# An mLSTM with two feed-forward layers: sign of the weight words placed by ScalarE, a finer order of steps, and the second layer's first pair in other banks

## Chip, cores, metric

One Trainium2 chip, one of its cores. The metric is the device time of one execution in microseconds (us), the median of the runs; the profile is of one execution.

## What is computed

Three stages follow each other, all in float32 with a precision that needs split products:

```python
# 1. a gated recurrence over 768 steps, 2 batches x 8 heads, head size 40
C = f * C + i * outer(v, k);  n = f * n + i * k
y = sigmoid(o) * (C @ q) / max(|n . q|, 1)
# 2. x: 1536 x 320 (all heads side by side)
h = max(max(x @ w1, x @ w2), x @ w3)        # 320 x 768 each
x = h @ w_out                                # 768 x 320
# 3.
h = x @ w_in                                 # 320 x 2048
g = h * tanh(softplus(h))                    # "mish"
out = g @ w_out2                             # 2048 x 320
```

The weights come in as 64-bit floats, two 32-bit words each; the kernel makes 32-bit floats of them on the chip.

## The kernel before

**Recurrence.** Steps are cut into 6 chunks of 128, times 2 batches: 12 units, numbered `u`, even units batch 0 and odd ones batch 1. A unit's steps have one-letter names: `F` spreads forget gates by TensorE into a PSUM bank, `D` scans them on VectorE into decays `dt`, `S` are the scores q.k (TensorE, `sc`), `X` multiplies both (VectorE), `V`, `K`, `Q` scale values, keys and queries (GpSimd or VectorE), `N` is the numerator (TensorE, `it`), `den`, `sg`, `xn` divide and gate, `T` transposes (`xp`), `xh` and `xl` are the high and low part of the result, which the first layer reads in three blocks of four units. `O` is the new part of the state (TensorE, `sp`), `sd` and `C` update the state `st`.

**First layer.** For each block, `P:blk,m,i` makes one of 18 products of 8 matmuls in the banks m0 to m2 (`mm`), `t` takes the maximum over three of them into `zraw` (ScalarE the first, VectorE the others), `hh` and `hl` split it; `d` multiplies by the output weights into the banks m0 to m2 (`mz`), `e` moves these out on ScalarE, two of them by L610 and the third by two moves to `sw` (L613, L614) and an addition on VectorE.

**Second layer.** For three blocks of 512 rows and 8 pairs of 128 columns each, `expand` makes the halves of a pair (`h`), `mish` evicts it twice on ScalarE (`gh`, `g`) with a subtraction on VectorE (`gl`), and two pairs later `contract` multiplies into four banks o0 to o3 (`o`).

**Weights.** A slab is 128 x 640 words of 64 bits: 9 slabs `w` (first layer), 3 `o`, 8 `i` and 8 `p` (second layer). `fet` loads a slab into one of three `raw` buffers, `sc` scales the two words on ScalarE (`dec` from the high word, and the low word in place), `mg` merges on VectorE in two instructions (L492 the digits, L494 the sign), `rd` rounds to the high part on ScalarE, `cut` makes the low part, on GpSimd or VectorE. The last five slabs (`LATE`: i7 and p4 to p7) are decoded while the second layer runs.

**Order.** `PLAN` is a written list of steps; it fixes the order on every engine and on SP's queue (all DMAs) up to the end of the first layer. Step names, numbers and, after @, the PSUM banks stand in it. From there a second fixed order holds for TensorE alone. Each engine works its queue in order, so whatever stands ahead in a queue must be finished first. PSUM banks c0, c1, s0, s1, s2 belong to the recurrence and become mx and o0 to o3 of the second layer when it is over. Where a step names no bank, `O` and `N` take s0. In `hbank` (L678) the pair's tiles `h` take mx for every fourth column and else m0, m1, m2 in turn, so the first pair takes m1 and mx.

The lines that matter below: L333 `D`, L352 `X`, L383 and L385 `N`, L465 `C`, L485 and L486 `sc`, L492 and L494 `mg`, L515 to L520 `rd`, L610 to L614 `e`, L678 `hbank`, L698 every matmul of the second layer.

Of the kernel before, what the change touches and what calls it, by code (L numbers as in the profile page):

```python
# [8 lines left out]
F32 = mybir.dt.float32  # L9
F32R = mybir.dt.float32r  # L10
AF = mybir.ActivationFunctionType
ALU = mybir.AluOpType
# [61 lines left out]
def mlstm_moe_kernel(ctx, tc, fi0, fir, qk2, q3, nat, w13, wo1, wi2, wo2, ident, bmask, out):  # L74
# [71 lines left out]
    def engine(dve):  # L146
        return nc.vector if dve else nc.gpsimd

# [155 lines left out]

    @step
    def _lf(u):
        c, b = divmod(u, B)
        nc.sync.dma_start(decays(u), dram_f[c - 2, b * H:(b + 1) * H].unsqueeze(0).to_broadcast([P, H, L]))
# [9 lines left out]
    @step  # L318
    def _F(u, *bs):
        c, b = divmod(u, B)  # L320
        src = fzs if c == 0 else fzr
        unit[u]["fp"] = [bank(t, f"fp{u}_{t}") for t in bs]
        for j, fp in enumerate(unit[u]["fp"]):
            for hh in range(4):
                r = b * H + 4 * j + hh
                nc.tensor.matmul(fp[:, hh * L:(hh + 1) * L], sel[:, r:r + 1].to_broadcast([P, P]), src, start=True, stop=True)
# [80 lines left out]
    @step  # L407
    def _xc(u):
        xn = unit[u]["xn"]
        nc.scalar.activation(xn[:, DM:3 * P], xn[:, 2 * P:DM], AF.Copy)  # L410
# [482 lines left out]
```

## Time and profile before

| | us |
|---|---|
| median of 3 runs | 390.83 (389.48 to 396.74) |
| the profiled execution | 391.06 |
| its span | 389.3 |

The span begins with the first instruction and ends with the last; 1.8 us lie around it. PE is TensorE's matmuls, PEld its weight loads, DVE VectorE, ACT ScalarE, POOL GpSimd, SPq the queue of DMA issues. A matmul's record lasts longer than its place in the pipeline, since the next one starts before its end.

### The profile page before, as it was taken

To read this page: it belongs to the slowest core of one execution; us is meant where nothing else is said; L and a number is where in the kernel's file an instruction comes from. 1 tells how busy PE (TensorE), PEld (TensorE's weight loads), DVE (VectorE), ACT (ScalarE), POOL (GpSimd) and SP (SyncE) were. 2 spreads that over 40 slices of the span, in tenths; PEclk is the share of its full clock that TensorE was granted. 3 is DMA by queue.
4 is the path that set the end of the run, shared out by engine and by line. 5 is a ranking of instruction groups with operands and counts; after the bars stand their busy time and mean duration, and the time that the engine had idled before them with its cause. 6 is when DMAs were issued, how large, how long until landed. Compare 5 with 4: busy or idle time off the path is not lost.

```text
span 389.3 us, 7460 instructions
## 1 busy us (share of the span) xinstructions
PE 373.9 (96%) x3001; PEld 325.0 (83%) x3001; DVE 201.4 (52%) x324; ACT 191.4 (49%) x385; POOL 120.1 (31%) x126
## 2 busy tenths in 40 slices
PE   8998997999999999999996899999999999999996
PEld 4986886888888888888884789999999998999985
DVE  7899999689996443236575345341221211312112
ACT  5698677562742420284668376562422423324231
POOL 6576774341332230255755322340010020000000
PEclk9999998799999999999999899999999999999999
DMA  6688886848766000001442800000100000200001
GB/s 177 211 280 253 251 249 216 282 144 259 247 203 226 14 2 0 2 0 67 136 134 69 338 2 0 2 3 2 69 2 0 2 2 2 69 2 2 0 3 67
DMA packets 15668, 38.80 MB, mean 100 GB/s; under 512 B 1886, under 2 KB 8515, under 8 KB 15635
## 3 DMA queue, kind: packets, MB, share of 16 engines
q1 hardware_dynamic: 15635, 38.34, 30.9%
q8 instruction: 23, 0.38, 0.4%
q14 instruction: 10, 0.08, 0.1%
HBM read 36.29 MB, written 2.04 MB: 98 GB/s over the span
## 4 chain that ended last, share of the span: by engine, by line
PE 88%; DVE 4%; ACT 4%; issue 2%; POOL 2%; POOLq 0%; DVEq 0%
PE h L698 22%; PE o L698 21%; PE mm L555 21%; PE it L385 5%; PE sc_c L346 2%; PE mz L597 2%; PE mz L599 2%; PE it L383 2%; PE mz L598 2%; PE fill L472 2%; PE sp L447 1%; PE mz L602 1%; PE mz L603 1%; PE xp L416 1%; DVE dec_w L494 1%
## 5 line engine op out<-in xcount | busy, mean ns | idle before, releaser
L698 PE MATMUL h<-zh,wi 64*128 64x512 f32 x480 | 87.5, 395 | 5.2 <-ACT zraw L610 4.8
L727 DVE TENSOR_TENSOR gl<-g,gh 128x512 fp32r<-128x512 f32 x48 | 34.2, 713 | 110.5 <-ACT g L726 110.5
L698 PE MATMUL o<-wo,gh 64*128 64x320 f32 (+1 forms) x736 | 89.8, 306 | 0.0
L698 PEld LDWEIGHTS o<-wo,gh 64*128 64x128 f32 (+1 forms) x736 | 85.4, 185 | 1.2 <-issue 0.4
L698 PE MATMUL o<-wo,gl 64*128 64x320 f32 (+1 forms) x368 | 84.5, 306 | 0.0
L698 PEld LDWEIGHTS h<-zh,wi 64*128 64x128 f32 x480 | 66.4, 188 | 13.6 <-ACT zraw L610 5.2
L555 PE MATMUL mm<-xh,w 128*128 128x512 f32 x270 | 72.8, 400 | 1.0 <-ACT xh L428 1.0
L725 ACT ACTIVATE gh<-h 128x512 fp32r<-128x512 f32 x48 | 28.9, 603 | 82.9 <-PE h L698 82.9
L698 PE MATMUL h<-zl,wi 64*128 64x512 f32 x240 | 68.8, 396 | 0.0
L698 PEld LDWEIGHTS o<-wo,gl 64*128 64x128 f32 (+1 forms) x368 | 68.0, 185 | 0.0
L555 PEld LDWEIGHTS mm<-xh,w 128*128 128x128 f32 x270 | 50.2, 191 | 11.8 <-ACT xh L428 1.3
L698 PEld LDWEIGHTS h<-zl,wi 64*128 64x128 f32 x240 | 42.9, 188 | 4.8
L555 PE MATMUL mm<-xl,w 128*128 128x512 f32 x162 | 45.6, 390 | 0.0
L573 DVE TENSOR_TENSOR zraw<-zraw,mm 128x512 f32<-128x512 f32 x36 | 24.5, 682 | 27.0 <-PE mm L555 26.8
L555 PEld LDWEIGHTS mm<-xl,w 128*128 128x128 f32 x162 | 30.5, 188 | 6.5
L635 POOL TENSOR_TENSOR zl<-zraw,zh 128x512 fp32r<-128x512 f32 x9 | 12.3, 1362 | 57.2 <-ACT zh L629 56.3
L726 ACT ACTIVATE g<-h 128x512 f32<-128x512 f32 x48 | 29.1, 606 | 0.0
L385 PE MATMUL it<-vp,dt 128*128 128x41 f32 x192 | 26.9, 283 | 0.0
L385 PEld LDWEIGHTS it<-vp,dt 128*128 128x128 f32 x192 | 25.8, 203 | 0.4
L578 ACT ACTIVATE hh<-zraw 128x512 fp32r<-128x512 f32 x18 | 11.3, 629 | 26.7 <-DVE zraw L573 26.7
L583 POOL TENSOR_TENSOR hl<-zraw,hh 128x512 fp32r<-128x512 f32 x11 | 15.6, 1421 | 20.0 <-ACT hh L578 14.8
L534 POOL TENSOR_TENSOR wo<-dec_p,wo 128x640 fp32r<-128x640 f32 x8 | 13.3, 1668 | 23.7 <-ACT wo L520 20.2
(157 smaller groups left out, 565.2 us busy)
## 6 DMA issues: line engine op xcount, KB each, us to landing
na<-in_nat_dram SPq DMA_DIRECT2D x12, 484.0 KB
raw_w<-in_w_dram SPq DMA_DIRECT2D x9, 640.0 KB
raw_i<-in_wi_dram SPq DMA_DIRECT2D x8, 640.0 KB
raw_p<-in_wo_dram SPq DMA_DIRECT2D x8, 640.0 KB
dt<-dram_f SPq DMA_DIRECT2D x8, 512.0 KB
qall<-in_qk_dram SPq DMA_DIRECT2D x24, 160.0 KB
raw_o<-in_wo_dram SPq DMA_DIRECT2D x3, 640.0 KB
out_dram<-ob SPq DMA_DIRECT2D x12, 160.0 KB
```

Source lines behind the costliest of these rows:

```text
L346: nc.tensor.matmul(scs[h % 2][:, (h // 2) * L:(h // 2 + 1) * L], qk[r:r + 64, 1, h // 2], qk[r:r + 64, 0, h // 2], start=True, stop=True)
L385: nc.tensor.matmul(it[:, h], t["dt"][:, h], vps[u % 2][:, h], start=(c == 0), stop=(c == 0 or h == h1 - 1))
L534: eng.tensor_tensor(w[:, 1], z, w[:, 0].bitcast(F32), op=ALU.subtract)
L555: nc.tensor.matmul(ups[blk, m, i], *seq[k], start=(k == 0), stop=(k == 7))
L573: nc.vector.tensor_tensor(top(blk, m), top(blk, m), ups[blk, m, i], op=ALU.max)
L578: nc.scalar.activation(hs[blk, m][0], top(blk, m), AF.Copy)
L583: engine(dve).tensor_tensor(ls, top(blk, m), h.bitcast(F32), op=ALU.subtract)
L635: nc.gpsimd.tensor_tensor(zl[:, j], zraw[:, j, t0:t0 + tb], zh[:, j].bitcast(F32), op=ALU.subtract)
L698: mm = nc.tensor.matmul(out_, a, r, start=first, stop=last).ins
L725: mark[blk, m] = nc.scalar.activation(gh, ps, AF.Mish)
L726: nc.scalar.activation(g, ps, AF.Mish)
L727: low[blk, m] = nc.vector.tensor_tensor(gl, g, gh.bitcast(F32), op=ALU.subtract)
```

## The change

1. `sc` scales the high word by ScalarE's Prelu with slope 2^32 for negative words, which leaves the sign where the shift by 3 puts it into bit 31. One merge is left per slab. The five late slabs keep the old form (`late`).
2. Steps become smaller or may take another engine: `F` for one bank each, `rd` and `cut` in two parts, copies (`dl`, `xc`, `rd`, `hh`, `C`) on ScalarE or VectorE by a flag.
3. `PLAN` is a new order throughout, with other banks; warm-up matmuls go from 23 to 15. The load of the mish table moves from the second block to the end of the plan.
4. `hbank` has a fixed pattern, in which the first pair of all takes o0 and o1, odd pairs m0 and mx, even ones m1 and m2.

```diff
-    "clear:4 first:0 clear:2 clear:0 first:1 clear:3 fill:9@c0 first:2 clear:6 lq:0 clear:1 ma:0 ln:0 clear:5 fa:0 clear:7 pick: ia:0 fe:0 ma:1 ie:0 ia:1 "
+    "clear:4 l3:2 clear:1 clear:0 first:0 clear:3 fill:9@m1 first:1 clear:5 ln:0 first:2 lq:0 fet:w,0 ma:0 lq:1 fa:0 fill:2@m0 ma:1 fe:0 fill:4@c1 clear:2 "
...
+    def copy(dve, a, b):
+        if dve:
+            nc.vector.tensor_copy(a, b)
+        else:
+            nc.scalar.activation(a, b, AF.Copy)
...
-    def _sc(k, g):
+    def _sc(k, g, late=0):
         raw = raws[k, g]
         decs[k, g] = stage.tile([P, 640], F32, tag="dec", bufs=2, name=f"dec_{k}{g}")
-        nc.scalar.activation(decs[k, g], raw[:, :, 1].bitcast(F32), AF.Copy, scale=2.0 ** -112)
+        if late:
+            nc.scalar.activation(decs[k, g], raw[:, :, 1].bitcast(F32), AF.Copy, scale=2.0 ** -112)
+        else:
+            nc.scalar.activation(decs[k, g], raw[:, :, 1].bitcast(F32), AF.Prelu, scale=2.0 ** -112, alpha=2.0 ** 32)
         nc.scalar.activation(raw[:, :, 0], raw[:, :, 0].bitcast(U32), AF.Copy, scale=15 * 2.0 ** -33)
...
-    def _mg(k, g, part):
+    def _mg(k, g, late=0):
         raw, b = raws[k, g], decs[k, g].bitcast(I32)
-        if part == 0:
-            nc.vector.scalar_tensor_tensor(b, b, 3, raw[:, :, 0], op0=ALU.logical_shift_left, op1=ALU.bitwise_or)
-        else:
+        nc.vector.scalar_tensor_tensor(b, b, 3, raw[:, :, 0], op0=ALU.logical_shift_left, op1=ALU.bitwise_or)
+        if late:
             nc.vector.scalar_tensor_tensor(b, raw[:, :, 1], -2147483648, b, op0=ALU.bitwise_and, op1=ALU.bitwise_or)
...
     def hbank(blk, m):
-        if m % 4 == 1:
-            return outp.tile([P, 512], F32, tag="mx", name=f"h2_{blk}_{m}")[:, 0:BLOCKS[blk][1]]
-        turn.append(m)
-        return bank(f"m{len(turn) % 3}", f"h2_{blk}_{m}")[:, 0:BLOCKS[blk][1]]
+        p, i = divmod(blk * KF2 + m, 2)
+        if p == 0 or (p % 2 and i):
+            return outp.tile([P, 512], F32, tag="mx" if p else f"o{i}", name=f"h2_{blk}_{m}")[:, 0:BLOCKS[blk][1]]
+        return bank("m0" if p % 2 else f"m{1 + i}", f"h2_{blk}_{m}")[:, 0:BLOCKS[blk][1]]
```

How instructions move is shown at three places. The first is VectorE's queue at the start of the recurrence, before: the scans `D` (`dt` from `fp`) and products `X` (`dt` from `sc`) of units 0 (`dt_174`) and 1 (`dt_234`).

```order
L333 SCALAR_TENSOR_TENSOR dt_174<-fp_s_156,idr 128x512
L333 SCALAR_TENSOR_TENSOR dt_174<-fp_s_155,idr 128x512
L272 SCALAR_TENSOR_TENSOR scr<-scr 16x128
L352 TENSOR_TENSOR dt_174<-sc_c_184,dt_174 128x4x128
L352 TENSOR_TENSOR dt_174<-sc_s_185,dt_174 128x4x128
L333 SCALAR_TENSOR_TENSOR dt_234<-fp_m_202,idr 128x512
L333 SCALAR_TENSOR_TENSOR dt_234<-fp_c_201,idr 128x512
```

The same place in the changed kernel, where unit 0 is `dt_106` and unit 1 `dt_107`:

```order
L279 SCALAR_TENSOR_TENSOR scr<-scr 16x128
L342 SCALAR_TENSOR_TENSOR dt_106<-fp_1_173,idr 128x512
L342 SCALAR_TENSOR_TENSOR dt_107<-fp_1_178,idr 128x512
L342 SCALAR_TENSOR_TENSOR dt_107<-fp_0_191,idr 128x512
L342 SCALAR_TENSOR_TENSOR dt_106<-fp_0_184,idr 128x512
L505 SCALAR_TENSOR_TENSOR dec_w_225<-dec_w_225,raw_w_137 128x640
L361 TENSOR_TENSOR dt_106<-sc_m_213,dt_106 128x4x128
L361 TENSOR_TENSOR dt_106<-sc_s_214,dt_106 128x4x128
```

All four scans of the two units now stand ahead of unit 0's products, and so does the merge of the first slab.

The second place is VectorE's queue in the first layer's first block, before, ahead of unit 4's state update (`st_97` from `sp_778`), whose bank unit 5's numerator takes next:

```order
L531 TENSOR_TENSOR w_5_733<-dec_w_682,w_5_733 64x128
L494 SCALAR_TENSOR_TENSOR dec_w_704<-raw_w_644,dec_w_704 128x640
L368 TENSOR_TENSOR kp_90<-na_724,dl_730 128x320
L352 TENSOR_TENSOR dt_607<-sc_c_784,dt_607 128x4x128
L492 SCALAR_TENSOR_TENSOR dec_w_795<-dec_w_795,raw_w_689 128x640
L352 TENSOR_TENSOR dt_607<-sc_c_785,dt_607 128x4x128
L333 SCALAR_TENSOR_TENSOR dt_771<-dt_771,eye 128x512
L465 SCALAR_TENSOR_TENSOR st_97<-sp_778,bmt,st_97 120x3x41 x2
```

And in the changed kernel, where the same update reads `sp_696`:

```order
L545 TENSOR_TENSOR w_6_737<-dec_w_703,w_6_737 128x512
L505 SCALAR_TENSOR_TENSOR dec_w_762<-dec_w_762,raw_w_701 128x640
L401 TENSOR_SCALAR den_782<-it_745 128x8
L402 TENSOR_TENSOR den_782<-den_782,it_745 128x8
L403 RECIPROCAL den_782<-den_782 128x8
L408 TENSOR_TENSOR sg_634<-sg_634,den_782 128x320
L414 TENSOR_TENSOR xn_803<-it_745,sg_634 128x320
L592 TENSOR_TENSOR zraw<-zraw,mm_3_1_772 128x512
L361 TENSOR_TENSOR dt_596<-sc_c_681,dt_596 128x4x128
L476 SCALAR_TENSOR_TENSOR st_97<-sp_696,bmt,st_97 120x3x41 x2
```

Of the sign merges none is left there; one merge, unit 4's division and a maximum stand ahead of the update. On TensorE the changed order has seven products, unit 4's numerator and its transposes between `O` and the numerator that takes its bank; before it has one product and a set of scores.

The third place is ScalarE's queue at the end of the first layer, before, with the moves of the last three banks `mz`:

```order
L610 ACTIVATE zraw<-mz_0_2036 128x512
L485 ACTIVATE dec_p_2122<-raw_p_2060 128x640
L486 ACTIVATE raw_p_2060<-raw_p_2060 128x640
L613 ACTIVATE sw_2125<-mz_2_2063 64x512
L614 ACTIVATE sw_2125<-mz_2_2063 64x512
L485 ACTIVATE dec_i_2129<-raw_i_2095 128x640
L486 ACTIVATE raw_i_2095<-raw_i_2095 128x640
L520 ACTIVATE wo_3_2134<-dec_p_2122 128x640
L610 ACTIVATE zraw<-mz_1_2079 128x512
```

And in the changed kernel:

```order
L499 ACTIVATE dec_p_2058<-raw_p_1948 128x640
L500 ACTIVATE raw_p_1948<-raw_p_1948 128x640
L499 ACTIVATE dec_i_2077<-raw_i_1993 128x640
L500 ACTIVATE raw_i_1993<-raw_i_1993 128x640
L154 ACTIVATE wi_2082<-dec_i_2077 128x512
L629 ACTIVATE zraw<-mz_0_2061 128x512
L632 ACTIVATE sw_2093<-mz_2_2044 64x512
L633 ACTIVATE sw_2093<-mz_2_2044 64x512
L629 ACTIVATE zraw<-mz_1_2016 128x512
L154 ACTIVATE wo_3_2097<-dec_p_2058 128x640
L664 ACT_TABLE_LOAD
```

The four moves now stand together, with the decoding of two slabs ahead of them and the table load behind. TensorE's own order has the first half of the first pair in pieces between the last products and the `mz` matmuls, since its banks o0 and o1 are free by then.

## Rows read from the trace of the kernel before

**Rows 1.** The page's busy times, shares of the span and instruction counts:

```profile
PE 373.9 (96%) x3001; PEld 325.0 (83%) x3001; DVE 201.4 (52%) x324; ACT 191.4 (49%) x385; POOL 120.1 (31%) x126
```

**Rows 2.** Whole-program waits of TensorE: engine, op, releaser, total us, times, longest:

```profile
PE h L698 <- ACT zraw L610: 4.8, 1, 4.8
PE it L383 <- DVE st L465: 2.6, 1, 2.6
```

**Rows 3.** Windows: stretch, length, busy by engine, granted clock, DMA share, GB/s:

```profile
0.00:10.00 10.00, 8.67 (x27) 4.21 (x29) 7.25 (x16) 5.69 (x14) 6.74 (x16) 1.00 0.68 179
20.00:30.00 10.00, 9.36 (x88) 8.34 (x86) 9.26 (x16) 9.86 (x27) 8.52 (x9) 1.00 0.83 261
60.00:70.00 10.00, 7.39 (x41) 6.60 (x38) 9.06 (x15) 7.28 (x16) 5.26 (x6) 0.76 0.72 239
70.00:80.00 10.00, 10.00 (x42) 8.17 (x40) 7.80 (x14) 5.94 (x13) 2.03 (x2) 0.89 0.88 259
200.00:220.00 20.00, 15.19 (x74) 12.12 (x74) 12.18 (x12) 12.18 (x23) 10.65 (x11) 0.91 0.47 160
```

**Rows 4.** Timeline of VectorE in the recurrence's start: start, us, what, [idle before]:

```profile
7.57 2.34 DVE L333 TENSOR_TENSOR_SCAN dt<-fp_s,idr 128x512 f32<-128x512 f32 x2 [1.18 <-PE fp_s L326]
...
12.37 0.69 DVE L352 TENSOR_TENSOR dt<-sc_c,dt 128x512 f32<-128x512 f32 x1 [1.63 <-ACT dl L338]
...
22.15 0.83 DVE L492 SCALAR_TENSOR_TENSOR dec_w<-dec_w,raw_w 128x640 int32<-128x640 int32 x1 [0.60 <-ACT raw_w L486]
...
32.55 0.48 DVE L405 TENSOR_TENSOR xn<-it,sg 128x320 f32<-128x320 f32 x1
```

**Rows 5.** Timeline of TensorE at the first product:

```profile
36.38 1.43 PE L555 MATMUL mm<-xh,w 128*128 128x512 f32 x5 [1.04 <-ACT xh L428]
```

**Rows 6.** Timeline of ScalarE: the wait for the identity, and a table load:

```profile
3.76 0.22 ACT L256 ACTIVATE sel<-idt 128x16 fp32r<-128x16 f32 x1 [1.75 <-DMA idt<-in_ident_dram]
...
7.42 1.28 ACT L373 ACT_TABLE_LOAD   x1
```

**Rows 7.** Chain that ended last, pieces from 70 us: start, us, what:

```profile
80.34 1.09 PE sc_c L346 x16
```

**Rows 8.** Timeline of TensorE, then VectorE, around the wait in the first block:

```profile
61.55 0.86 PE L555 MATMUL mm<-xl,w 128*128 128x512 f32 x3
65.02 0.52 PE L383 MATMUL it<-st,cb 120*128 120x123 f32 x2 [2.61 <-DVE st L465]
...
64.09 0.78 DVE L465 SCALAR_TENSOR_TENSOR st<-sp,bmt,st 120x123 f32<-120x123 f32 x3
```

**Rows 9.** Timeline of TensorE, then of ScalarE, between the two layers:

```profile
209.99 0.39 PE L603 MATMUL mz<-hl,wo 128*128 128x512 f32 x1
...
209.28 0.60 ACT L610 ACTIVATE zraw<-mz 128x512 f32<-128x512 f32 x1
...
214.55 0.59 ACT L610 ACTIVATE zraw<-mz 128x512 f32<-128x512 f32 x1
```

**Rows 10.** Chain that ended last, from the second layer's start:

```profile
215.19 7.13 PE h L698 x46
...
229.94 3.49 PE h L698 x30
```

**Rows 11.** Instructions by form: count | busy us, mean ns | idle before:

```profile
L494 DVE SCALAR_TENSOR_TENSOR dec_i<-raw_i,dec_i 128x640 int32<-128x640 int32 x8 | 11.7, 1469 | 0.1
L492 DVE SCALAR_TENSOR_TENSOR dec_i<-dec_i,raw_i 128x640 int32<-128x640 int32 x8 | 7.0, 881 | 2.2 <-ACT raw_i L486 1.8 <-issue 0.4
L485 ACT ACTIVATE dec_w<-raw_w 128x640 f32<-128x640 f32 x9 | 7.1, 792 | 4.8 <-POOL w L531 4.2 <-DVE w L531 0.6
```

**Rows 12.** Timeline of VectorE, then of GpSimd: a sign merge beside a cut:

```profile
45.80 1.80 DVE L494 SCALAR_TENSOR_TENSOR dec_w<-raw_w,dec_w 128x640 int32<-128x640 int32 x1
...
45.38 1.53 POOL L529 TENSOR_TENSOR w<-dec_w,w 128x512 fp32r<-128x512 f32 x1 [2.29 <-ACT w L515]
```

More of the change, by code (lines that the diff above doesn't have):

```diff
@@ L303, in decays @@
         return unit[u]["dt"]
+    for u in range(DB):
+        decays(u)
     @step
@@ L318, in _F @@
     @step
-    def _F(u, *bs):
+    def _F(u, j, tag):
         c, b = divmod(u, B)
         src = fzs if c == 0 else fzr
[L322 to L326, printed above, removed]
+        fp = unit[u]["fp", j] = bank(tag, f"fp{u}_{j}")
+        for hh in range(4):
+            r = b * H + 4 * j + hh
+            nc.tensor.matmul(fp[:, hh * L:(hh + 1) * L], sel[:, r:r + 1].to_broadcast([P, P]), src, start=True, stop=True)
     @step
@@ L330, in _D, with _dl @@
         t = unit[u]
-        dt = decays(u) if "dt" not in t else t["dt"]
+        dt = t["dt"]
         half = dt.rearrange("p h t -> p (h t)")[:, j * 512:(j + 1) * 512]
-        nc.vector.tensor_tensor_scan(half, *((t["fp"][j], idr) if "fp" in t else (half, eyes[0])), 0.0, op0=ALU.mult, op1=ALU.add)
+        nc.vector.tensor_tensor_scan(half, *((t["fp", j], idr) if ("fp", j) in t else (half, eyes[0])), 0.0, op0=ALU.mult, op1=ALU.add)
     @step
-    def _dl(u):
+    def _dl(u, dve=0):
         unit[u]["dl"] = a2.tile([P, H, 1], F32, tag="dl", name=f"dl{u}")
-        nc.scalar.activation(unit[u]["dl"], unit[u]["dt"][:, :, L - 1:L], AF.Copy)
+        copy(dve, unit[u]["dl"], unit[u]["dt"][:, :, L - 1:L])
     @step
@@ L407, in _xc @@
     @step
-    def _xc(u):
+    def _xc(u, dve=0):
         xn = unit[u]["xn"]
-        nc.scalar.activation(xn[:, DM:3 * P], xn[:, 2 * P:DM], AF.Copy)
+        copy(dve, xn[:, DM:3 * P], xn[:, 2 * P:DM])
     @step
@@ L457, in _C @@
     @step
-    def _C(u):
+    def _C(u, dve=0):
         c, b = divmod(u, B)
@@ L461, in _C @@
         for j in range(3):
-            if c == 0:
+            if c == 0 and dve:
+                nc.vector.tensor_scalar(st[b][:, j::3], sp[:, j:H:3], bmt[:, j:j + 1], None, op0=ALU.mult)
+            elif c == 0:
                 nc.scalar.activation(st[b][:, j::3], sp[:, j:H:3], AF.Copy, scale=bmt[:, j:j + 1])
@@ L510, in _rd @@
     @step
-    def _rd(k, g):
+    def _rd(k, g, part, dve=0):
         w, z = slab(k, g), decs[k, g]
@@ L514, in _rd, with _cut @@
             z = z.rearrange("p (s f) -> p s f", f=P)
-            nc.scalar.activation(w[:, 0:4], z[:, 0:4], AF.Copy)
-            nc.scalar.activation(w[0:64, 8], z[0:64, 4], AF.Copy)
-            nc.scalar.activation(w[64:128, 9], z[64:128, 4], AF.Copy)
+            if part == 0:
+                copy(dve, w[:, 0:4], z[:, 0:4])
+            else:
+                copy(dve, w[0:64, 8], z[0:64, 4])
+                copy(dve, w[64:128, 9], z[64:128, 4])
         else:
             z = z.rearrange("p (k f) -> p k f", k=2)
-            nc.scalar.activation(w[:, 0] if k == "p" else w[:, :, 0:DM], z, AF.Copy)
+            copy(dve, w[:, 0] if k == "p" else w[:, :, 0:DM], z)
     @step
-    def _cut(k, g, dve=0):
+    def _cut(k, g, part, dve=0):
         eng = engine(dve)
@@ L528, in _cut @@
             t = z[:, 4]
-            eng.tensor_tensor(w[:, 4:8], z[:, 0:4], w[:, 0:4].bitcast(F32), op=ALU.subtract)
-            eng.tensor_tensor(w[64:128, 8], t[0:64], w[0:64, 8].bitcast(F32), op=ALU.subtract)
-            eng.tensor_tensor(w[0:64, 9], t[64:128], w[64:128, 9].bitcast(F32), op=ALU.subtract)
+            if part == 0:
+                eng.tensor_tensor(w[:, 4:8], z[:, 0:4], w[:, 0:4].bitcast(F32), op=ALU.subtract)
+            else:
+                eng.tensor_tensor(w[64:128, 8], t[0:64], w[0:64, 8].bitcast(F32), op=ALU.subtract)
+                eng.tensor_tensor(w[0:64, 9], t[64:128], w[64:128, 9].bitcast(F32), op=ALU.subtract)
         elif k == "p":
@@ L538, in _cut @@
             z = z.rearrange("p (k f) -> p k f", k=2)
-            eng.tensor_tensor(w[:, :, 320:384], z[:, :, 256:320], w[:, :, 256:320].bitcast(F32), op=ALU.subtract)
-            eng.tensor_tensor(w[:, :, 384:640], z[:, :, 0:256], w[:, :, 0:256].bitcast(F32), op=ALU.subtract)
+            if part == 0:
+                eng.tensor_tensor(w[:, :, 320:384], z[:, :, 256:320], w[:, :, 256:320].bitcast(F32), op=ALU.subtract)
+            else:
+                eng.tensor_tensor(w[:, :, 384:640], z[:, :, 0:256], w[:, :, 0:256].bitcast(F32), op=ALU.subtract)
     XB = 512
@@ L575, in _hh @@
     @step
-    def _hh(blk, m):
+    def _hh(blk, m, dve=0):
         hs[blk, m] = [m1.tile([P, XB], F32R, tag=f"{t}{m}", bufs=1, name=f"{t}{blk}_{m}") for t in ("hh", "hl")]
-        nc.scalar.activation(hs[blk, m][0], top(blk, m), AF.Copy)
+        copy(dve, hs[blk, m][0], top(blk, m))
     @step
@@ L674, in mlstm_moe_kernel @@
     low = {}
-    turn = []
     def hbank(blk, m):
-        if m % 4 == 1:
-            return outp.tile([P, 512], F32, tag="mx", name=f"h2_{blk}_{m}")[:, 0:BLOCKS[blk][1]]
-        turn.append(m)
-        return bank(f"m{len(turn) % 3}", f"h2_{blk}_{m}")[:, 0:BLOCKS[blk][1]]
+        p, i = divmod(blk * KF2 + m, 2)
+        if p == 0 or (p % 2 and i):
+            return outp.tile([P, 512], F32, tag="mx" if p else f"o{i}", name=f"h2_{blk}_{m}")[:, 0:BLOCKS[blk][1]]
+        return bank("m0" if p % 2 else f"m{1 + i}", f"h2_{blk}_{m}")[:, 0:BLOCKS[blk][1]]
     issued = []
@@ L784, in ahead @@
             with tc.issue_after(mark[0, m - 1].ins), tc.issue_after(low[0, m - 1].ins):
-                follow(f"sc:{n} mg:{n},0 mg:{n},1 rd:{n} cut:{n}")
+                follow(f"sc:{n},1 mg:{n},1 rd:{n},0 cut:{n},0" + (f" rd:{n},1 cut:{n},1" if n[0] == "i" else ""))
     def pair_of(blk, p):
```

63 rows, old and new, of the table PLAN are left out of this document.

## The prediction

> **What bounds the kernel now.** I read the page's busy times first. TensorE is busy for 96% of the span, no other engine for more than 52% [rows 1], so what can be won lies in the time in which TensorE waits, or runs slowly. Then I read the list of TensorE's waits, where two stand out behind the first product: 2.6 us for VectorE's `st` and 4.8 us for ScalarE's `zraw` [rows 2]. Last the windows, because a wait costs more than its own length: the granted clock is 1.00 at the start, 0.76 and 0.89 in the two stretches of 10 us that hold and follow the first wait, and 0.91 in the 20 us around the second [rows 3].
>
> The reader is to see four losses. (a) The first product starts at 36.38 [rows 5]; until then TensorE runs the recurrence and fills, and ScalarE (9.86 busy of 10) and VectorE (9.26) set the pace [rows 3]. (b) In the first block the numerator of unit 5 waits 2.61 for `C`, whose last piece starts at 64.09 and takes 0.78 [rows 8]. It wants the bank that `C` has to read, and `C` stands in VectorE's queue behind merges and maxima, as the second place of the order shows. (c) Between the layers TensorE ends its last `mz` at 209.99 plus 0.39 and starts `h` at 215.19. The first pair's bank m1 is released by ScalarE's last L610, 5.27 later than its first, at 214.55, since the decoding of two slabs stands between these moves [rows 9]. (d) The clock behind both waits. In the windows of (b), at 1.2 GHz instead of 2.4 for part of them, (1 − 0.76) · 10 + (1 − 0.89) · 10 = 3.5 us are lost. In that of (c), (1 − 0.91) · 20 = 1.8; the chain agrees, for 46 matmuls of `h` take 7.13 there and 46/30 · 3.49 = 5.35 later on [rows 10].
>
> **The change part by part.** The sum is made against the profiled execution, 391.06 (span 389.3 and 1.8 around it); the median of the runs is 390.83, 0.2 less.
>
> *The wait between the layers.* The first pair goes to o0 and o1, which belonged to the recurrence and are free well before the last `mz`; its products stand in pieces among block 2's last ones, so no move releases them. The next pair needs m0, which comes free with the first of four moves that now stand together, at 0.60 each [rows 9], while TensorE still has parts of two pairs' `h` ahead that need no move, of 3.49 a pair [rows 10]. So the wait goes, 4.8, and with it the slow clock, 1.8. What is late next is the first `mish` on ScalarE: the table load, 1.28 where the trace has one [rows 6], stands directly behind the moves; 4 · 0.60 + 1.28 = 3.7 is covered by the 3.49 of a pair to within 0.2, which I put at nothing, because two pairs of `h` come before the first `contract`. If that cover is gone, the price is 0.2 to 1.3.
>
> *The wait in the first block.* In the new order TensorE has seven products between unit 4's `O` and the numerator that follows in its bank, against one product and a set of scores; the last three matmuls of one product start at 61.55 and take 0.86 [rows 8], and eight of them some 2 us. So `C` has about 12 us more, and this wait goes, 2.6, with its 3.5 of clock.
>
> *The sign merges.* Of 23 slabs L494 goes: 1.47 us on average for the slabs of `i`, against 0.88 for L492 [rows 11]. VectorE thus loses some 20 to 34 us of work, but pays for TensorE only where VectorE is late: before the first product and in the first block. Prelu in place of Copy is not in the trace. Its bounds are the Copy's price, 0.79 [rows 11], and twice that; above, three slabs before the first product would cost 2.4 on a ScalarE that is 98% busy there [rows 3]. Below nothing is excluded, for it does the Copy's work on the same tile and more. I take nothing extra, by the nearest row, the Copy itself.
>
> *The start.* VectorE's idle time for `dl`, 1.63, and for the first slab, 0.60 [rows 4], goes, because four scans now stand ahead of unit 0's products: −2.2. The loads of `na`, `l3` and the gates are put ahead of the identity in SP's queue, and `sel` already waits 1.75 for it [rows 6]; at 179 GB/s [rows 3] their roughly 760 KB are 4.2 us in the worst case and nothing in the best. I take 0.6, near the lower end, because `F` also needs the gates from ScalarE's queue, which come later than `sel`. From the end of the last `xn` (32.55 + 0.48 = 33.03) to the first product are 3.35 [rows 4, 5]; 1.04 of it is TensorE's wait for `xh`, which the order covers with unit 4's scores: 2.3 remain. First product at 33.03 − 2.2 + 0.6 + 2.3 = 33.7, so 2.7 earlier; the scores, 1.09 [rows 7], are then done as well: gain 3.8. At the best the identity costs nothing, one sign merge of about 1.1 leaves VectorE's start and half of the 2.3 goes: 30.9, gain 6.6. At the worst identity and Prelu eat it: 0.
>
> *New stalls.* The order is new everywhere, and in the first 120 us VectorE is as full as 9.06 of 10 in the window of the first wait, with slabs landing at 239 to 261 GB/s [rows 3]. VectorE takes over copies from ScalarE (`rd`, `hh`, `xc`, `dl` by flag), three of 128x512 in the first block, so a part of what L494 leaves is filled again. No row shows where the next gap of TensorE falls. Bounds: nothing, or two like (b), 2 · (2.6 + 3.5) = 12.2. I take one, 6.1, the nearest row: in a block whose supply is so tight one wait with its clock is the rule of this trace.
>
> **Sum.** 391.06 − 3.8 (start) − 6.1 (first block) − 6.6 (between the layers) + 6.1 (one new stall) = 380.7, let us say 380.5.
>
> **A rule against it.** A sign merge beside GpSimd's cut took 1.80, from 45.80, while the cut ran from 45.38 for 1.53; a merge of the same shape with no cut beside it takes 0.83 [rows 4, 12]. So VectorE and GpSimd hold each other up, by about 1.0 here. The Trainium skill, "SBUF — State Buffer", section "Who interferes with whom", has it that VectorE copies in a two-port mode, and its instructions with two SBUF inputs, exclude GpSimd's reads for a whole instruction. The row agrees for two inputs; no row shows a copy. By that rule the new copies would wait as the merges did, which makes the second rival below.
>
> **The rivals.**
> 1. *A second new stall in the first block.* VectorE, or the arrival of slabs, holds TensorE twice. For it: VectorE at 9.06 and DMA at 0.72 to 0.88 of their windows while TensorE waits [rows 3]. Against: the sign merges are gone. 380.5 + 6.1 = 386.6.
> 2. *VectorE's copies are held up by GpSimd's cuts.* 1.0 each [rows 12], three in the first block on the way to a product: 380.5 + 3.0 = 383.5. Against: GpSimd has only 5.26 of 10 there [rows 3].
> 3. *The change of banks doesn't do what it says.* ScalarE reaches the moves late, since the decoding of two slabs stands ahead of all four, about 3.0 by rows 9; TensorE's next pair still waits and its clock still falls. 380.5 + 6.6 = 387.1. Against: parts of two pairs of `h` lie between.
> 4. *Slower than before: the clock falls in the start.* There are 8 fills fewer and no product yet; the wait of 2.61 in the first block cost the clock, whereas the start with its fills kept 1.00 [rows 3, 8]. If TensorE falls to 1.2 GHz before the first product and each short wait of the start keeps it there, work of up to 20 us takes twice its time: up to 400.5. It ends slower than before from 10.6 us lost. Against: busy time in the start came from the recurrence more than from fills, and VectorE sets the pace there, so that TensorE has slack for a slow clock.
>
> **How the numbers follow.** Forecast 0.62, second stall 0.14, held-up copies 0.10, banks 0.08, slow start 0.06. The range reaches from 391.06 − 6.6 − 6.1 − 6.6 = 371.8 (best start, no new stall) to 391.06 − 12.7 + 12.2 = 390.6 (no gain in the start, two stalls): 372 to 390, with some 0.05 below and 0.08 above. 2% of 390.83, about what a measurement of this kernel can tell from no change, are the bounds 383.0 and 398.6. Below 383.0 lie 0.56 of the forecast's 0.62, half of the copies' 0.10 and 0.05 of the first and third rival, 0.66 in all; above 398.6 lies most of the slow start, 0.05; 0.29 between.
>
> **What would show it.** First product (L574) at 33.7, between 30.9 and 36.4; later than 36.4 speaks for the slow start, with a granted clock under 1.00 before 40 us. In TensorE's waits no `h` for `zraw`, and 1.00 in 200 to 220 us; if 4 to 5 us stand there again, the banks did nothing. No wait of `it` for `st` of 2 us near 60; a new one, of whatever name, with a clock near 0.76 behind it, is the stall that I put in, two of them the first rival. Prelu rows near 0.79. VectorE's 128x512 copies near 0.6 to 0.7, or over 1.2 beside cuts for the second rival. A pair of `h` still at 3.49. What would make the forecast wrong: no new stall at all (374.4), or a first product that is no earlier.

## The result, and the profile after

| | before | after |
|---|---|---|
| median, us | 390.27 (389.48 to 396.74, 4 runs) | 376.81 (376.0 to 377.77, 4 runs) |
| profiled execution | 391.06 | 377.48 |
| its span | 389.3 | 375.7 |
| first product starts | 36.38 | 35.68 |

The ratio is 0.966, with a 95% interval from 0.962 to 0.970: faster by 13.5 us. The forecast was 380.5 in a range from 372 to 390. Ratios here leave out, on both sides, executions that took over 1.5% more than the fastest of their kernel; the kernel before scatters more than the changed one (beside the experiments its executions lie between 388.7 and 399.1, but for one of 940.56), and those from 394.5 us on have a mean granted clock of 0.957 to 0.970, the shorter ones of 0.970 to 0.991.

The page's busy times of the changed kernel, which answer to [rows 1]:

```profile
PE 367.9 (98%) x2993; PEld 318.9 (85%) x2993; DVE 198.8 (53%) x344; ACT 175.6 (47%) x353; POOL 100.2 (27%) x111
```

TensorE's share rose from 96% to 98%; VectorE's work hardly fell (201.4 to 198.8), since the copies that it took over, and the finer steps, fill most of what the sign merges left. The whole-program waits of TensorE, which answer to [rows 2]:

```profile
PE it L394 <- DVE dt L361: 1.6, 1, 1.6
PE fill L483 <- DVE zraw L162: 1.2, 1, 1.2
PE it L392 <- DVE cb L372: 0.7, 1, 0.7
```

Both large waits of before are gone. What is left lies before the first product, but for 0.7 us on `cb` in the first block. The windows, which answer to [rows 3]:

```profile
10.00:20.00 10.00, 8.43 (x68) 8.07 (x66) 8.84 (x14) 7.90 (x15) 7.22 (x11) 0.77 0.91 275
20.00:30.00 10.00, 10.00 (x93) 9.37 (x92) 7.53 (x15) 7.87 (x20) 7.14 (x8) 0.89 0.58 179
...
60.00:70.00 10.00, 10.00 (x55) 8.52 (x55) 9.86 (x15) 9.06 (x21) 7.75 (x8) 1.00 0.59 184
70.00:80.00 10.00, 9.27 (x63) 7.73 (x63) 9.80 (x15) 6.20 (x12) 7.18 (x7) 1.00 0.65 193
...
200.00:220.00 20.00, 19.98 (x167) 16.53 (x167) 8.01 (x14) 12.51 (x22) 1.36 (x2) 1.00 0.42 159
```

From 60 to 80 and from 200 to 220 us the granted clock is 1.00, where before it was 0.76, 0.89 and 0.91. In its place the slow stretch lies in the start now: 0.77 and 0.89 from 10 to 30 us, where before had 1.00 in its profile. TensorE's timeline shows why:

```profile
15.02 3.20 PE L394 MATMUL it<-vp,dt 128*128 128x41 f32 x16 [1.57 <-DVE dt L361]
...
23.00 1.98 PE L394 MATMUL it<-vp,dt 128*128 128x41 f32 x16
...
35.68 1.42 PE L574 MATMUL mm<-xh,w 128*128 128x512 f32 x5
```

Unit 0's numerator waits 1.57 us for VectorE's `X`, and right behind it 16 matmuls of the same form that take 1.98 at 23.00 (unit 1's) take 3.20; the granted clock from 16 to 20 us is 0.50, that of 1.2 GHz. Between the layers, TensorE's last `mz` and the `h` behind it, with a weight load (PEld), then ScalarE's moves (compare [rows 9]):

```profile
205.22 0.39 PE L618 MATMUL mz<-hl,wo 128*128 128x512 f32 x1
205.54 0.50 PE L715 MATMUL h<-zh,wi 64*128 64x512 f32 x2
...
206.30 0.73 PE L715 MATMUL h<-zh,wi 64*128 64x512 f32 x4
...
206.30 0.30 PEld L715 LDWEIGHTS h<-zh,wi 64*128 64x128 f32 x4 [0.46 <-ACT zraw L629]
...
205.65 0.60 ACT L629 ACTIVATE zraw<-mz 128x512 f32<-128x512 f32 x1 [4.26 <-PE mz L618]
...
208.74 1.28 ACT L664 ACT_TABLE_LOAD   x1
210.05 0.60 ACT L742 ACTIVATE gh<-h 128x512 fp32r<-128x512 f32 x1
```

`h` follows `mz` at once. ScalarE has done its decoding by then and itself waits 4.26 us for the last `mz`; before, it came to the moves late. The margin is small: at 206.30 begins the next pair, whose bank m0 the first move frees at 206.25 (205.65 + 0.60), and its weight load waits for that move. The chain there, compare [rows 10]:

```profile
206.30 7.11 PE h L715 x60
213.41 3.52 PE o L715 x48
216.94 3.42 PE h L715 x30
```

60 matmuls take 7.11 where 46 took 7.13. A pair's step stays what it was: 3.42 + 3.52 = 6.94 against 3.49 + 3.45.

**Where the 13.6 us of span went.** The first product comes 0.7 earlier, and from there to the end the span has 340.0 instead of 352.9, 12.9 less. In these 12.9: unit 4's scores, now ahead of the first product, 1.1; the wait in the first block with its clock, 2.6 + 3.5 = 6.1; the wait between the layers with its clock, 4.8 + 1.8 = 6.6; a new wait in the first block, 0.7 given back; and the pieces of `h` among the products, about 1.1 given back (shown under the old banks below). That is 12.0; a wait of 0.4 for `g` behind the first pairs is gone too, and the last 0.5 I haven't followed.

### The profile page after: what moved, and what is told of

It is laid out like the page before. It is cut to its first block, busy times and chain, and to the rows that moved or that the text cites. A ratio compares the mean times of both kernels' runs of the same rounds, so it can differ in the third digit from the quotient of the medians.

```text
span 375.7 us, 7421 instructions
## 1 busy us (share of the span) xinstructions
PE 367.9 (98%) x2993; PEld 318.9 (85%) x2993; DVE 198.8 (53%) x344; ACT 175.6 (47%) x353; POOL 100.2 (27%) x111
## 4 chain that ended last, share of the span: by engine, by line
PE 93%; DVE 3%; DMA 2%; issue 1%; ACT 1%; SPq 0%; DVEq 0%; ACTq 0%
PE mm L574 25%; PE o L715 23%; PE h L715 22%; PE it L394 6%; PE mz L618 2%; PE mz L616 2%; PE mz L617 2%; PE it L392 2%; PE sc_c L355 2%; PE sp L456 2%; PE mz L621 1%; DMA cp<-dram_c 1%; PE mz L622 1%; PE xp L425 1%; DVE dt L342 1%
## 5 line engine op out<-in xcount | busy, mean ns | idle before, releaser
L715 PE MATMUL o<-wo,gh 64*128 64x320 f32 (+1 forms) x736 | 85.0, 306 | 0.0
L715 PE MATMUL h<-zh,wi 64*128 64x512 f32 x480 | 75.2, 390 | 0.0
L715 PEld LDWEIGHTS o<-wo,gh 64*128 64x128 f32 (+1 forms) x736 | 65.0, 185 | 2.2 <-issue 0.4
L715 PE MATMUL o<-wo,gl 64*128 64x320 f32 (+1 forms) x368 | 59.3, 306 | 0.0
L715 PEld LDWEIGHTS h<-zh,wi 64*128 64x128 f32 x480 | 44.0, 185 | 9.3 <-ACT zraw L629 0.5
L715 PE MATMUL h<-zl,wi 64*128 64x512 f32 x240 | 47.3, 391 | 0.0
L715 PEld LDWEIGHTS o<-wo,gl 64*128 64x128 f32 (+1 forms) x368 | 36.1, 185 | 0.0
L715 PEld LDWEIGHTS h<-zl,wi 64*128 64x128 f32 x240 | 22.5, 184 | 5.3 <-issue 0.4
L590 ACT ACTIVATE zraw<-mm 128x512 f32<-128x512 f32 x18 | 10.7, 592 | 21.8 <-PE mm L574 21.7
L342 DVE TENSOR_TENSOR_SCAN dt<-dt,eye 128x512 f32<-128x512 f32 x16 | 19.1, 1206 | 0.0
```

The costliest lines, as they stand in the source:

```text
L342: nc.vector.tensor_tensor_scan(half, *((t["fp", j], idr) if ("fp", j) in t else (half, eyes[0])), 0.0, op0=ALU.mult, op1=ALU.add)
L590: nc.scalar.activation(top(blk, m), ups[blk, m, 0], AF.Copy)
L715: mm = nc.tensor.matmul(out_, a, r, start=first, stop=last).ins
```

## Experiments

Ratios compare with the kernel before. The first four undo or add one part, to see whether the parts act alone. The start scatters between executions, so the table splits each profiled one at its first product.

| profiled execution of | time, us | first product | from there to the end |
|---|---|---|---|
| the kernel before | 391.06 | 36.38 | 352.9 |
| before, new banks | 389.61 | 34.73 | 353.1 |
| before, one merge | 394.68 | 40.05 | 352.9 |
| before, other bank | 391.44 | 40.22 | 349.5 |
| before, banks and moves | 392.60 | 35.31 | 355.5 |
| before, all together | 388.09 | 37.60 | 348.7 |
| the changed kernel | 377.48 | 35.68 | 340.0 |
| the changed kernel again | 377.38 | 35.59 | 340.0 |
| changed, old banks | 379.98 | 34.29 | 343.9 |
| changed, two merges | 393.47 | 36.84 | 354.9 |
| changed, fills | 375.00 | 33.22 | 340.0 |
| changed, merge later | 377.36 | 35.53 | 340.1 |
| changed, merge later and fills | 377.01 | 35.22 | 340.0 |
| changed, fills again | 385.14 | 43.69 | 339.7 |

The new banks, the other bank, and banks and moves leave the order of the old start alone, and yet its first product lies at 34.73, 40.22 and 35.31.

**The new banks alone, in the kernel before.** `hbank` of the changed kernel, nothing else:

```diff
-        if m % 4 == 1:
-            return outp.tile([P, 512], F32, tag="mx", name=f"h2_{blk}_{m}")[:, 0:BLOCKS[blk][1]]
-        turn.append(m)
-        return bank(f"m{len(turn) % 3}", f"h2_{blk}_{m}")[:, 0:BLOCKS[blk][1]]
+        p, i = divmod(blk * KF2 + m, 2)
+        if p == 0 or (p % 2 and i):
+            return outp.tile([P, 512], F32, tag="mx" if p else f"o{i}", name=f"h2_{blk}_{m}")[:, 0:BLOCKS[blk][1]]
+        return bank("m0" if p % 2 else f"m{1 + i}", f"h2_{blk}_{m}")[:, 0:BLOCKS[blk][1]]
```

> The kernel before with the new bank pattern of the second layer alone; PLAN and the sign merges as before. Theory (banks): the first pair no longer waits for ScalarE's last move, so the wait of 4.8 us goes and with it the slow clock behind it, 1.8: 390.3 - 6.6 = 383.7 (382.5 to 385), clock 1.00 in 200 to 220 us. Rival (moves): the decoding between the moves holds the next pair as well, so that banks alone do little without the four moves being put together: 387 to 391.

Measured: 390.87 median, ratio 0.997 (0.993 to 1.001): no difference, and none from the first product on (353.1 against 352.9). TensorE's waits, then the chain from ScalarE's decoding to `h`:

```profile
PE h L696 <- SPq L694: 2.3, 1, 2.3
```

```profile
216.88 0.35 ACT raw_i L486
...
219.23 0.45 SPq L479
...
219.80 5.30 PE h L696 x30
```

The wait for `zraw` is gone, but 2.3 us later in the pair SP's queue (SPq) holds TensorE. When the two halves of the rows change places within a pair, `together` lets an empty instruction on SP wait for the first half and TensorE for that instruction; it stands in SP's queue behind five slab loads, of which the first waits for ScalarE's L486 to free the buffer. And the clock falls behind this wait too (0.91 from 220 to 240 us). Neither theory had this: the banks do release the pair, and late decoding still holds it by another way. These 2.3 + 1.8 leave 2.5 of the 6.6 to be gained; they went into the pieces:

```profile
182.80 1.45 PE L555 MATMUL mm<-xh,w 128*128 128x512 f32 x5
...
185.29 1.42 PE L555 MATMUL mm<-xh,w 128*128 128x512 f32 x5
...
197.37 1.30 PE L555 MATMUL mm<-xh,w 128*128 128x512 f32 x5
...
199.18 1.30 PE L555 MATMUL mm<-xh,w 128*128 128x512 f32 x5
```

With the new banks the 16 matmuls of the first pair's first half stand in seven pieces among the products. A product with a piece behind it takes 2.5 (182.80 to 185.29), one without 1.8. From the first product to the last `mz` it is 178.7 us instead of 173.6, so the 16 cost 5.1, where 16 in a row take 16/30 · 3.49 = 1.9.

**The old banks, in the changed kernel** (the same diff the other way):

> The changed kernel with the old bank pattern of the second layer. Theory (banks): the first pair takes m1 and mx again and waits for the last of four moves that stand together, 4 x 0.60 = 2.4 us plus some tenths, and the clock falls behind it, 1.5 to 1.8: 376.8 + 4.2 = 381.0 (379 to 383). Rival (moves): with the moves put together the banks hardly matter, wait under 1 us and no loss of clock: 376.5 to 378.

Measured: 380.93 (379.98 to 382.07), 4.1 above the changed kernel. The wait and the window between the layers:

```profile
PE h L717 <- ACT zraw L629: 2.5, 1, 2.5
```

```profile
200.00:220.00 20.00, 17.15 (x140) 13.93 (x140) 7.55 (x13) 10.79 (x19) 0.46 (x1) 0.91 0.44 165
```

2.5 of wait, which is the four moves, and (1 − 0.91) · 20 = 1.8 of clock: 4.3. The banks theory holds here, though two terms that it leaves out stand against each other. With the old banks no piece of `h` stands among the products: from the first product to the last `mz` it is 167.3 us instead of 169.5 in the changed kernel. In the changed kernel twelve matmuls of the first pair cost these 2.2 and four more 0.7 behind the last `mz`, together 2.9, where 16 in a row take 1.8: the pieces cost about 1.1. And a wait of 0.3 for `g` is back. In the changed kernel the banks are worth 4.1 (3.9 from the first product on), and in the kernel before next to nothing.

**One merge, in the kernel before.** Prelu for the 23 early slabs, the second merge left out, order and banks as before:

```diff
-        nc.scalar.activation(decs[k, g], raw[:, :, 1].bitcast(F32), AF.Copy, scale=2.0 ** -112)
+        if f"{k}{g}" in LATE.values():
+            nc.scalar.activation(decs[k, g], raw[:, :, 1].bitcast(F32), AF.Copy, scale=2.0 ** -112)
+        else:
+            nc.scalar.activation(decs[k, g], raw[:, :, 1].bitcast(F32), AF.Prelu, scale=2.0 ** -112, alpha=2.0 ** 32)
```

> The kernel before with Prelu and one merge for the 23 early slabs; PLAN and banks as before. Theory (VectorE's queue): the sign merges ahead of C in the first block, six of about 1 us, are what made the numerator wait; without them that wait of 2.6 and its 3.5 of clock go: 384.2 (382 to 386). Rival (order): the queue shifts but the same places wait for GpSimd's cuts or for slabs instead; 388 to 391. Prelu rows: 0.79 as for Copy, or above 0.9 if it costs more.

Measured: 396.15, ratio 1.015 (1.008 to 1.021): no gain; whether it is slower stays open. VectorE behind unit 5's scores in the first block, then TensorE:

```profile
64.10 0.69 DVE L352 TENSOR_TENSOR dt<-sc_c,dt 128x512 f32<-128x512 f32 x1 [0.70 <-PE sc_c L346]
...
67.17 0.78 DVE L465 SCALAR_TENSOR_TENSOR st<-sp,bmt,st 120x123 f32<-120x123 f32 x3
...
68.10 0.46 PE L383 MATMUL it<-st,cb 120*128 120x123 f32 x2 [1.98 <-DVE st L465]
```

VectorE now waits for the scores, yet `C` starts 3.07 behind the first product `X` (3.06 before), since two products, one merge and a scan stand between in the queue, and TensorE has one product of 2 us meanwhile. So the wait is 2.0 instead of 2.6: most of it was made by the order, and the sign merges added 0.6; the clock behind it still falls (0.97 and 0.69 from 60 to 80 us). From the first product to the end it takes as long as before, 352.9. The loss lies in the start, with the clock at 0.74 and 0.58 from 10 to 30 us:

```profile
20.00:30.00 10.00, 10.00 (x66) 8.98 (x66) 6.48 (x10) 5.39 (x14) 4.22 (x6) 0.58 0.70 246
```

TensorE has a wait of 1.3 for `kp` there, but that this wait or this edit brought the clock down is not shown. With banks and moves below, the same place has this wait and the clock stays 1.00:

```profile
PE it L385 <- POOL kp L368: 1.2, 1, 1.2
...
10.00:20.00 10.00, 8.59 (x85) 7.92 (x85) 8.55 (x16) 6.94 (x15) 5.74 (x8) 1.00 0.67 206
```

In the kernel with another bank (also below) the old start, unedited, has its first product at 40.22, with 0.83, 0.92 and 0.57 in the three windows from 10 to 40 us. And all four executions here (394.68 to 396.32) have a mean clock of 0.961 to 0.965, as the kernel before has in its executions from 394.5 us on.

Prelu itself costs nothing: the nine scalings of `w` average 788 ns against 792 for Copy [rows 11].

**Two merges, in the changed kernel** (`late = 1` set at the head of `_sc` and `_mg`):

> The changed kernel with the old two merges for every slab (sign by VectorE, straight behind the digits), order otherwise as it is. Theory (VectorE's queue): VectorE is 93 to 98% busy from 40 to 80 us, so nine to twelve more merges of 0.8 to 1.5 us come back on the path, with at least one loss of clock: 376.8 + 9 = 386 (381 to 392). Rival (order does it): 376.5 to 379.

Measured: 394.37 (393.47 to 395.92), 17.6 above the changed kernel, 1.2% above before (0.3% to 2.1%) and above the theory's range: the changed order can't live without the one merge. TensorE's waits:

```profile
PE it L392 <- DVE cb L372: 4.5, 2, 2.7
PE h L717 <- SPq L715: 2.7, 1, 2.7
PE mm L576 <- DVE zraw L594: 1.9, 1, 1.9
PE it L394 <- DVE dt L361: 1.7, 1, 1.7
```

VectorE is late for numerators, a product and the start alike, and between the layers there is a wait for SP's queue, as with the new banks alone.

**Another bank for the numerator, in the kernel before**, so that it need not wait for `C`:

```diff
-    ... mg:w,7,1 N:5 ln:7 ... fet:o,1 T:4 sd:5 ...
+    ... mg:w,7,1 N:5@s1 ln:7 ... fet:o,1 T:4@s0 sd:5 ...
```

> The kernel before with unit 5's numerator in s1 and unit 4's transposes in s0, so that the numerator no longer needs the bank that C reads; all queues keep their order. Theory (the bank held by C): the wait of 2.61 us and the clock behind it (0.76 and 0.89 in the windows 60 to 80) go, 6.1 in all, or 5 if the transposes wait some tenths: 390.3 - 5.6 = 384.7 (383.5 to 386.5) in an execution whose start keeps its clock. Rival (supply): TensorE waits for VectorE's X or for a slab there all the same, 1.5 to 2.5 us under another name: 388 to 391.

Measured: 389.92, ratio 0.994 (0.989 to 0.998), some 2.5 us gained where 5.6 were expected; the shortest execution, 387.92, is above the theory's range too. The wait in the first block:

```profile
PE mm L555 <- DVE zraw L573: 1.8, 1, 1.8
```

Mostly the rival: 1.8 us come back as a product that waits for VectorE's maximum to free its bank, ten microseconds later, though here the clock stays 1.00. Between the layers the clock falls deeper behind the same wait of 4.8, to 0.83 from 200 to 220 us instead of 0.91, which is 1.6 more: 6.1 − 1.8 − 1.6 = 2.7. From the first product on the profiled execution gains 3.4, and it loses 3.8 in the start.

**Banks and moves, in the kernel before**: the new `hbank`, and `e:2,0 e:2,2 e:2,1 ea:2` taken from between the decoding to behind `sc:p,3`, `sc:i,6` and their merges (but for the last, the sign of i6).

> The kernel before with the new bank pattern and the four moves put together behind the decoding of the two slabs (no part of the decoding between them). With the banks alone 2.3 us of wait were left, for SP's queue, which was held by the load of a slab whose buffer ScalarE freed only after the moves. Theory (queues): with the decoding ahead, the buffer and so SP come free earlier and no wait over 0.5 us is left between the layers, clock 1.00 from 200 to 240 us: 6.6 less than before, 383.5 to 385 in an execution whose start keeps its clock. Rival: the next wait is for the table load or for the slab itself, 387 to 390.

Measured: 394.36, ratio 1.010 (1.000 to 1.020), and 2.6 more from the first product on. ScalarE before the first move, then TensorE's wait:

```profile
217.38 0.79 ACT L485 ACTIVATE dec_i<-raw_i 128x640 f32<-128x640 f32 x1 [1.26 <-POOL wi L531]
...
218.72 0.59 ACT L610 ACTIVATE zraw<-mz 128x512 f32<-128x512 f32 x1
```

```profile
PE h L696 <- ACT zraw L610: 3.6, 1, 3.6
```

Both theories fail: the decoding ahead of the moves waits for GpSimd's cut and makes the moves themselves late; TensorE, whose first half of the first pair is used up in pieces among the products, has no `h` left that needs no move. With the decoding in front, the moves come in time only if ScalarE is early, as in the changed kernel, where it waited 4.26 for `mz`.

**All of it together, in the order of before**: one merge, the other bank, banks and moves, and `fill:6@m1` ahead of `N:0`.

> The kernel before, in its own order, with all that was tried alone put together: Prelu and one merge for the 23 early slabs, unit 5's numerator and unit 4's transposes in other banks, the new bank pattern with the moves together, and six warm-up matmuls ahead of unit 0's numerator. Theory (the parts only work together): no wait of over 1 us behind the first product: 378 to 382. Rival (the order itself is what counts): waits of VectorE and of GpSimd's cuts in the first block come back under other names: 384 to 390.

Measured: 384.9 (384.23 to 388.09), ratio 0.984 (0.976 to 0.992). TensorE's waits over 0.8 us behind its fills:

```profile
PE h L699 <- ACT zraw L613: 2.9, 1, 2.9
...
PE sc_s L346 <- DMA qall<-in_qk_dram: 0.9, 2, 0.7
```

The time is in the rival's range, but not by the rival's waits: in the first block nothing is left of the wait that one merge alone left at 2.0 and the bank alone moved elsewhere as 1.8: it takes both (the fills and the moves act at other places). Between the layers 2.9 and a clock of 0.83 in 200 to 220 us remain, some 6 of the 8.7 us that separate its profiled execution from the changed kernel behind the first product (348.7 and 340.0). That execution, 388.09, is the longest of the four; the others, 384.23 to 385.39, have a mean clock of 0.994 to 0.998 instead of 0.987, so much of the clock's part is not in them.

**Fills in the changed kernel's start.** Seven warm-up matmuls where the numerator waits:

```diff
-    D:2,1 N:0 lq:3
+    D:2,1 fill:7@c0 N:0 lq:3
```

> The changed kernel with seven more warm-up matmuls (fill:7@c0) ahead of unit 0's numerator, where TensorE waits 1.57 us for VectorE's X. Theory (clock in the start): that wait makes the clock fall from 15 to 22 us (0.77 and 0.89 in the windows 10 to 20 and 20 to 30), which costs 10 x 0.23 + 10 x 0.11 = 3.4 us on the way to the first product; with the wait filled the clock stays 1.00, the first product starts at 32.5 to 33.5 instead of 35.75 and the time is 376.8 - 2.8 = 374.0 (373 to 375). Rival (VectorE sets the start): the chain of the start runs over VectorE and ScalarE, TensorE's speed there is slack: first product within 0.7 of 35.75, 376 to 378.

> The changed kernel with the first slab's merge (0.80 us) behind unit 0's products X on VectorE instead of ahead of them, and the slab's first rounding behind unit 1's dl. Theory (VectorE's queue): the numerator starts 0.8 us earlier, the wait before it falls from 1.57 to 0.8, and the clock falls later or not at all: 373 to 376. Rival: the clock falls all the same and the 0.8 is lost again at the next wait: 376 to 377.5.

> The changed kernel with the merge later and four fills in what is left of the wait. Theory: both gains, clock 1.00 throughout, first product at 32 to 33: 373.2 (372 to 374.5), better than both. Rival: no better than fills alone, since other waits of the start take the 0.8 back: 374 to 375.

In the first of these, the executions took 374.55, 375.0, 383.36 and 387.28; the profiled one, 375.0, shows TensorE so:

```profile
15.24 1.88 PE L394 MATMUL it<-vp,dt 128*128 128x41 f32 x16
...
33.22 1.45 PE L574 MATMUL mm<-xh,w 128*128 128x512 f32 x5
```

The clock is 1.00 in all windows up to 240 us and the first product starts at 33.22, as expected: 2.5 us earlier, though the numerator itself starts 0.2 later than without fills. The chain of the start does run over TensorE, and the clock's price there is real; from the first product on both take 340.0. The merge later alone gave 377.5 (377.23 to 377.81, clock 0.78 and 0.88 as before it), the rival: behind 1.2 us of wait the clock fell as well. Merge later with four fills gave 376.19 (375.49 to 377.01), clock 0.91 and 0.92, the first product at 35.22: neither theory nor rival; four fills were too few, 0.8 of wait was left.

**The fills again, beside the changed kernel itself.**

> The changed kernel itself, on the chip and in the rounds of the next one. Both theories: 376 to 377.8, clock 0.77 to 0.9 in the window 10 to 20.

> The seven added warm-up matmuls again, in the rounds of the one before. Theory (clock in the start): 374.5 to 375.2 where the clock stays 1.00, 1.5 to 2.5 less than the changed kernel. Rival: the two executions of 383 and 387 show that the fills bring the clock down elsewhere in about half of the cases, so that nothing is won on average.

The changed kernel: 377.35 (376.08 to 378.88, 6 runs), ratio 0.963 (0.958 to 0.969). With fills: 374.99 and 375.76, but four executions of 382.83 to 385.14. So of ten executions with fills four gain about 2 us and six lose 5 to 10. One of the six was profiled (385.14); TensorE's longest wait for a load in it, its first product, and a window:

```profile
PE sc_s L355 <- DMA qall<-in_qk_dram: 1.3, 1, 1.3
```

```profile
43.69 1.43 PE L574 MATMUL mm<-xh,w 128*128 128x512 f32 x5
```

```profile
30.00:40.00 10.00, 10.00 (x50) 9.63 (x50) 3.42 (x11) 3.47 (x9) 0.12 (x1) 0.50 0.70 245
```

Running ahead, TensorE meets queries and keys of units 2 and 3 that have not landed, loses the clock there, and stays at 1.2 GHz until past 40 us. The lead alone does not explain it. In the execution of 375.0, about as far ahead, the last of these loads held TensorE for 0.2; the first line is from that one, the second from the one of 385.14:

```profile
22.84 0.34 PE L355 MATMUL sc_c<-qall 64*128 64x128 f32 x1 [0.17 <-DMA qall<-in_qk_dram]
...
25.98 0.55 PE L355 MATMUL sc_c<-qall 64*128 64x128 f32 x1 [0.93 <-DMA qall<-in_qk_dram]
```

The load came 3.1 later here, and why is not shown. The changed kernel comes to the same tile at 25.27 and has no wait for it; a load as late as this one would have held it for 0.7. None of the three variants is a version to keep: the merge later alone gains nothing, with four fills at most about 1 us, and for the seven fills the rival is right, on the whole nothing is won. That the load comes late in the other five is not shown, for only one was profiled.

## Why the prediction held, and where it failed

**Between the layers (6.6):** right in size, in part for another reason. The wait and its clock went, and so did the "cover" step: with the table load behind the moves, the first `mish` starts at 210.05 and TensorE has no wait for it. But "parts of two pairs' `h` ahead that need no move" is wrong. TensorE's order goes to the next pair, and so to m0, after the first half of the first, and behind the last `mz` only 0.7 us of `h` were left of that half: enough for the first move of 0.60, and no more. It fitted because ScalarE stood waiting, 4.26 early; that is what made the third rival fail, and why ScalarE was early no run isolates. Where ScalarE was late, the same banks left 3.6 of wait. The pieces among the products, put at no cost, cost about 1.1 in the changed kernel. And banks were put first: alone, in the kernel before, they bring nothing (353.1 against 352.9 from the first product on), because SP's queue holds the pair and the pieces cost more there.

**The first block (6.1):** right in size: the wait of 2.6 and its clock are gone. That seven products between `O` and the numerator do it is not shown alone. One merge alone left 2.0, another bank alone 1.8, both together none, clock 1.00; and the new order without the one merge has waits of 4.5 for `cb` and 1.9 for `zraw`. So the order and the one merge are both needed.

**The sign merges:** Prelu at nothing extra was right, 786 ns for `w` in the changed kernel against 792. That VectorE's work pays only where VectorE is late was said of the start and the first block; putting the merges back cost 17.6, and some 4.5 of it lies between the layers, in the wait for SP's queue (2.7) and a clock of 0.91 from 220 to 240 us.

**The start (3.8): this term failed.** It measured 1.8 between the two profiles, and not even that is sure: with its order unedited the old start has its first product at 34.73, 35.31, 36.38 and 40.22, the new one at 34.29, 35.59 and 35.68. The first product came at 35.68 instead of 33.7. VectorE's scans do stand ahead as expected, but the first slab's merge stands there too, and TensorE's 1.57 of wait for `X` brought its clock down. That is the fourth rival in small: (1 − 0.77) · 10 + (1 − 0.89) · 10 = 3.4 us, where that rival was priced at up to 20. Its premise, that the start before keeps 1.00, holds for the profile before but not for every execution. With the clock kept, the first product of the changed kernel is at 33.22.

**The new stall (6.1): mis-sized and misplaced.** It was put into the first block, where only 0.7 was found, with no loss of clock. What there was of it, a wait of 1.57 and 3.4 of clock, lay in the start. The two misses have opposite signs, −2.0 and +5.4, and their sum of 3.4 is most of the distance between 380.5 and 376.8. That the forecast came so near is in part luck.

**The second rival**, VectorE's copies held up by GpSimd, did not show where it was put: the 128x512 copies of `w` took 0.42 us each, below the 0.6 to 0.7 I took for the least, and no GpSimd instruction ran beside them. The rule behind it did show on copies of 8 columns, 0.17 otherwise: in the changed kernel one took 0.69 and one 0.36. VectorE first, then GpSimd:

```profile
74.88 0.69 DVE L152 COPY dl<-dt 128x8 f32<-128x8 f32 x1
...
74.47 1.07 POOL L408 TENSOR_TENSOR sg<-sg,den 128x320 f32<-128x320 f32 x1 [0.85 <-ACT sg L382]
```

And in the kernel with two merges:

```profile
83.02 1.25 DVE L152 COPY dl<-dt 128x8 f32<-128x8 f32 x1
...
82.38 1.86 POOL L604 TENSOR_TENSOR hl<-zraw,hh 128x512 fp32r<-128x512 f32 x1
```

The copies ended at 75.57 and 84.27, just behind GpSimd's instructions (74.47 + 1.07 = 75.54 and 82.38 + 1.86 = 84.24). That is what the Trainium skill says ("SBUF — State Buffer", section "Who interferes with whom": the one that is issued second is blocked for the other's whole instruction).

## What to carry to other kernels

Price a wait of the busiest engine with the slow clock behind it, and ask what is late next before counting it as won: of three single repairs and a pair of them in the old order none gained over 1%, and in the new one the same parts were worth 4 and 18 us, for a part counts only when whatever would wait next has been moved as well. Where the start scatters, split the executions behind it, here at the first product, before comparing. Filling a small wait with warm-up work lost more often than it won, six times of ten; the one loss that was profiled ran into loads that had not landed.

## What the runs showed of the hardware

- TensorE's clock fell to 1.2 GHz behind waits of 0.8, 1.2 and 1.6 us in the changed kernel's start, but stayed at 1.00 through 1.2 on `kp` in the old start (banks and moves), through the 0.7 in the first block, and through the 1.8 on `zraw` in the kernel with the other bank. So the length of a wait alone doesn't decide it.
- Matmuls of 64 rows (`h`) put in seven pieces among products of 128 rows cost TensorE 5.1 us, where the same 16 in a row take 1.9.
- VectorE's copy of 128x512 from SBUF to SBUF takes 0.42 us, where ScalarE's takes 0.63 (the changed kernel).
